# Sparse attention in front of a mixture of experts: mask added by the array, one exponential for all tiles, sums by VectorE, operands built by chunks of features

## The chip, the cores and the metric

One core of one Trainium2 chip. The time is microseconds on the device from the launch to the end of the kernel; the table below has the median of three runs of the kernel before. One execution was profiled: all rows of the trace come from it.

## The reference, cut to what matters

```python
# q, k, v: (4, 8, 576, 64) f32, stride = 32
scores = (1/sqrt(D)) * q @ k^T
mask_local   = (rel >= 0) & (rel < 32)                 # heads 0..3, rel = query position - key position
mask_strided = (rel >= 0) & (kpos % 32 == qpos % 32)   # heads 4..7
scores = where(mask, scores, -1e9); scores -= max(scores); attn = exp(scores)
attn  /= sum(attn) + 1e-9
x = (attn @ v), heads side by side: (2304, 512)
P = exp(x @ w_gate - max); 8 rounds of division by row sums and column sums   # gate, 8 experts
y = sum over experts e of P[:, e] * (relu(x @ w1[e]) @ w2[e])                 # 512 -> 1024 -> 512
out = elu(y @ w_in) @ w_out                                                   # 512 -> 2048 -> 512
```

## The kernel before, in words

**Attention.** The eight heads of a batch are taken in four pairs, two local, two strided, in the order local, strided, local, strided, and each pair is two units: 32 units over the four batches. A unit has 4 to 6 tiles. A local tile has 128 rows (64 queries of two heads) against 96 keys; a strided tile has 108 rows against 54 keys. Only tiles that the mask leaves non-empty are computed; inside a tile the mask is a table of 0 and -1e9 (m_local, m_str). There are 160 tiles in all.

A unit goes through four stages, each a generator: att_s1 (once per pair) turns q and k by TensorE transposes (L425), ScalarE copies q with the scale (L437), VectorE copies k (L443). att_s2 makes the scores of all tiles of a unit in one bank of PSUM (L470: every f32 matmul stands in the trace as two weight loads and two matmuls), VectorE adds the mask on the way to SBUF (L484) and takes the negated maximum (L487). Deferred behind it are exps, one ScalarE exponential per tile with the maximum as bias and the sum accumulated (L491), and norm, two small VectorE operations for the reciprocal (L495, L496) and a GpSimd multiplication of the whole unit (L497). att_s3 transposes the weights in two groups (L511) and copies them out of PSUM (L514 on ScalarE, L516 on VectorE). att_s4 multiplies by v (L529) and VectorE copies the result into x (L549).

The function attention runs a loop over u; in one loop stand att_s2 of unit u-2, a half of att_s1, att_s4 of unit u-5, the other half of att_s1, and the two groups of att_s3 of unit u-4, in this order. After each of these steps the program yields, and a yield counts down the deferred work: exps is written into the program four yields behind its att_s2 (DEF_EXP = 3), norm six (DEF_NORM = 5). Each engine runs its instructions in the order in which they were written; other engines' results are waited for by semaphores. While only attention runs (loops 0 to 20; loops 0 and 1 hold att_s1 alone), nearly every second bank that is opened gets one 512-column matmul on data that nobody reads (warm_up, L341: the first nine banks, then each with n % WARM_MOD < WARM_OF, WARM_MOD = 2).

**Start of the experts.** At u = MOE_FROM = 21 the experts begin, and from there on one step of attention stands in each gap between groups of matmuls. The first layer (gemm1, L923) is a Winograd form of Strassen's product over seven products of quarters. Its operands are made of x's halves: quarters B11 and B21 of the first 512 tokens (build_a), and B22 and the differences T1 to T4 that also need the next 512 tokens (build_b: four VectorE subtractions at L267 for each of two 128-feature chunks, c = 0 and 1). Each operand is split into a high part (ScalarE cast, L277 or L158) and the rest (a subtraction at L168, on VectorE for c = 0 and GpSimd for c = 1 in most of build_b, the other way round in build_a), and a product is three matmuls per chunk. build_a is queued when batch 0's attention is done (batch_done(0), at the end of loop 12); build_b when batch 1's is done, in loop 21, so behind the first step of the experts. A build step is taken at every second yield while attention runs alone, and in each gap later; need(x) in gemm1 writes build steps until operand x is written. The preparation of expert weights (GpSimd sums at L186, casts and subtractions at L158 and L168) begins at yield 66 and takes every second one.

Behind the attention (230 us) the kernel goes on with both layers' matmuls (L923, L1072) to the end; the change touches nothing that is written there but the form of the entries in the set built.

Of the kernel before, what the change touches and what calls it, by code (L numbers as in the profile page):

```python
# [75 lines left out]
def sparse_attention_moe_kernel(ctx: ExitStack, tc: tile.TileContext, a, out):  # L76
# [178 lines left out]
    def build_b(a, b, home=None):  # L255


        hi, lo = xb

        def minus(x, y, i, c):  # L260
            if home:
                out = home(i, c)
            elif i == 4:
                out = y
            else:
                out = hp_.tile([P, HALF], F32, tag="hh" if c else "hl", name="t")
            ve.tensor_tensor(out=out, in0=x, in1=y, op=ALU.subtract)  # L267
            return out

        t1 = [minus(b(c), a(c), 1, c) for c in (0, 1)]  # L270
        yield True
        t2 = [minus(b(c + 2), t1[c], 2, c) for c in (0, 1)]
        yield True

        def both(x, t, engs):
            for c in (0, 1):
                se.copy(hi[:, x, c], t[c])  # L277
            yield True
            for c in (0, 1):
                low(hi[:, x, c], lo[:, x, c], t[c], engs[c])  # L280
            built.add(x)
            yield True

        yield from both(T2, t2, (ve, ve))
        yield from both(T1, t1, (ve, po_))
        t3 = [minus(t2[c], a(c), 3, c) for c in (0, 1)]
        yield from both(T3, t3, (ve, po_))

        t4 = [minus(a(c + 2), t2[c], 4, c) for c in (0, 1)]
        yield from both(T4, t4, (ve, po_))  # L290
        b22 = [b(c + 2) for c in (0, 1)]
        yield from both(B22, b22, (ve, ve))

    def build_plain(src, hi, lo, tmp):
# [158 lines left out]
    def att_s2(u):  # L453
        m, hf = divmod(u, 2)
        local, tiles, nq, nk = geometry(u)
        nt = len(tiles)
        t = pst[m]
        s = ust[u] = {}
        e = s["e"] = at_p.tile([P, 5 * LK], F32, tag="e", name="e_t", bufs=3)[:nq, : nt * nk].rearrange(
            "p (t k) -> p t k", k=nk  # L460
        )
        ng = st_p.tile([P, 6], F32, tag="ng", name="ng")[:nq, :nt]
        sm = st_p.tile([P, 6], F32, tag="sm", name="sm")[:nq, :nt]
        pp = warm_up(abank())
# [12 lines left out]
        s3 = pp[:nq, : nt * nk].rearrange("p (t k) -> p t k", k=nk)  # L477
        if local:
            parts = [(0, 1, m_local[:, 0:1, :])] if hf == 0 else []
            parts.append((len(parts), nt, m_local[:, 1:2, :]))  # L480
        else:
            parts = [(0, nt, m_str[:nq, None, :])]
        for i0, i1, mask in parts:
            ve.tensor_tensor(  # L484
                out=e[:, i0:i1], in0=s3[:, i0:i1], in1=mask.to_broadcast([nq, i1 - i0, nk]), op=ALU.add
            )
        ve.tensor_reduce(out=ng, in_=e, axis=AX.X, op=ALU.max, negate=True)  # L487

        def exps():
            for i in range(nt):  # L490
                se.activation(e[:, i], e[:, i], AF.Exp, bias=ng[:, i : i + 1], accum_out=sm[:, i : i + 1])  # L491

        def norm():
            rc = st_p.tile([P, 6], F32, tag="rc", name="rc")[:nq, :nt]
            ve.tensor_scalar_add(rc, sm, EPS)  # L495
            ve.reciprocal(rc, rc)  # L496
            po_.tensor_tensor(out=e, in0=e, in1=rc[:, :, None].to_broadcast([nq, nt, nk]), op=ALU.mult)  # L497

        defer(DEF_EXP, exps)
        defer(DEF_NORM, norm)  # L500
        yield True

    def att_s3(u):
        local, tiles, nq, nk = geometry(u)
        s = ust[u]
        s["eT"] = at_p.tile([LK, 6 * 2 * SG], F32, tag="eT", name="eT")
        for i0 in (0, 3):
            n = min(3, len(tiles) - i0)
            pt = warm_up(ybank())
            for i in range(n):  # L510
                pe.transpose(pt[:nk, i * nq : (i + 1) * nq], s["e"][:, i0 + i], ident[:nq, :nq])  # L511
            dst = s["eT"][:nk, i0 * nq : (i0 + n) * nq]
            if i0 and not local:
                se.copy(dst, pt[:nk, : n * nq])  # L514
            else:
                ve.tensor_copy(dst, pt[:nk, : n * nq])  # L516
            yield True

    def att_s4(u):
# [57 lines left out]
    def gate_block():  # L577

        for half, parts in enumerate((((B11, 0), (B21, 2)), ((B11, 0), (T1, 0), (B22, 2)))):
            while not all(x in built for x, _ in parts):  # L580
# [53 lines left out]
    def batch_done(b):  # L634

        if b == 0:
            po_.tensor_copy(x1_[:, :, : S - HALF], x0_[:, :, HALF:])
            start_build((0, False, "a"), build_a(lambda c: x0_[:, c, :HALF]))
            gates.append(gate_block())
        elif b == 1:  # L640
            start_build((0, False, "b"), build_b(lambda c: x0_[:, c, :HALF], lambda c: x1_[:, c, :HALF]))
            gates.append(gate_tile(NA // P, x1_[:, :, HALF:]))

    def pair_done(m):

        b, hp = pair_of(m)
        t0 = max(NA, b * S)
        if t0 < (b + 1) * S:
            nc.sync.dma_start(out=x_late[hp][:, t0 - NA : (b + 1) * S - NA], in_=xs[b][hp][:, t0 - b * S :])
        if b > 1:  # L650
            gates.append(gate_pair(b, m % KD, hp))
# [23 lines left out]
        while any(x[0] == key for x in builds):  # L675
            build_step()

    def need(x):
        while x not in built:
            assert builds  # L680
            build_step()

    def attention():
# [1 line left out]
            return stage(u) if 0 <= u < NU else iter(())  # L685

        s1 = iter(())
        for u in range(NU + 5):
# [5 lines left out]
            if u - 5 == 2 * H:  # L694
                batch_done(1)
# [12 lines left out]
            w = u - 5  # L708
# [6 lines left out]
            if w == H - 1:  # L715
                batch_done(0)


    load_qk(0)
# [247 lines left out]
    def gemm1(sg, p, early=False):  # L967
# [356 lines left out]
```

## Time and profile before

| | |
|---|---|
| median of 3 runs | 2082.65 us (2076.6 to 2087.6) |
| the profiled execution's own time | 2084.41 us |
| its span, first to last instruction | 2082.6 us |
| mean granted TensorE clock over the span | 0.986 |
| attention alone | from 9.0 us (first scores) to 95.1 us (first matmul of the experts) |
| attention beside the experts | 95.1 to about 230 us |

Engines: PE = TensorE matmul, PEld = TensorE weight load, DVE = VectorE, ACT = ScalarE, POOL = GpSimd. A PE instruction's end is modelled, so the distance between starts tells more than a duration. The granted clock is 1.00 at the chip's higher TensorE level, 2.4 GHz, and 0.50 at the lower, 1.2 GHz.

### The profile page before, as it was taken

Reading aid. Unit: us, or ns where it says so; the run is one execution under the profiler, and the core shown is the slowest. Engines: PE = TensorE matmul, PEld = TensorE weight load, DVE = VectorE, ACT = ScalarE, POOL = GpSimd, SP = SyncE. Lnnn points to the kernel's source line nnn. Section 1 sums busy time; section 2 is a strip of 40 time slices with the busy share of each in tenths; the row PEclk is TensorE's granted clock in tenths of the full one; section 3 lists DMA queues with packets and bytes.
Section 4 is the critical chain, followed back from the end, with each engine's and each line's share of the span. In section 5 each row is a group of like instructions: output and inputs, shape, how many; then the busy total and the mean of one; then the engine's idle time right before and its main releaser. Section 6 shows DMA issues by size and latency. Waiting matters only on the chain.

```text
span 2082.6 us, 26962 instructions
## 1 busy us (share of the span) xinstructions
PE 2034.9 (98%) x10196; PEld 1687.3 (81%) x10196; DVE 1310.0 (63%) x2165; ACT 743.3 (36%) x1707; POOL 633.7 (30%) x709
## 2 busy tenths in 40 slices
PE   9989999999999999999999999999999989998999
PEld 7767788888888888788888888888888868886887
DVE  5767775645545556666666666666664475557665
ACT  6746333223322323322222222222222354444543
POOL 1422333233333334322222222222222322224231
PEclk8889999999999999999999999999999999999999
DMA  9632121111111213122222222222211101122111
GB/s 179 144 68 74 53 71 51 51 51 55 57 41 51 62 51 111 62 76 85 73 85 73 86 72 86 73 85 73 85 63 44 41 21 41 41 81 91 41 51 51
DMA packets 143378, 143.12 MB, mean 69 GB/s; under 512 B 67328, under 2 KB 106128, under 8 KB 143248
## 3 DMA queue, kind: packets, MB, share of 16 engines
q1 hardware_dynamic: 142288, 141.20, 23.1%
q8 instruction: 80, 1.31, 0.3%
q14 instruction: 50, 0.41, 0.1%
q10 hardware_dynamic: 960, 0.21, 0.1%
HBM read 123.55 MB, written 20.19 MB: 69 GB/s over the span
## 4 chain that ended last, share of the span: by engine, by line
PE 90%; DVE 5%; ACT 4%; issue 1%; POOL 0%; DVEq 0%; ACTq 0%; POOLq 0%
PE ybank L1072 45%; PE bank L923 39%; DVE xl L168 1%; ACT g L946 1%; PE bank L470 1%; ACT g L945 1%; PE ybank L529 1%; PE ybank L511 1%; PE ybank L470 1%; ACT e_t L491 1%; DVE u L982 1%; ACT hh L950 1%; PE bank L425 0%; PE ybank L589 0%; DVE c L982 0%
## 5 line engine op out<-in xcount | busy, mean ns | idle before, releaser
L1072 PE MATMUL ybank<-w2h,hh 128*128 128x512 f32 x1280 | 504.0, 394 | 9.6 <-DVE acc L1089 8.2
L1072 PE MATMUL ybank<-w2h,hl 128*128 128x512 f32 x1280 | 499.2, 390 | 0.0
L1072 PE MATMUL ybank<-w2l,hh 128*128 128x512 f32 x1280 | 499.0, 390 | 0.0
L923 PE MATMUL bank<-xh,w1h 128*128 128x512 f32 x1120 | 443.9, 396 | 10.3 <-DVE u L982 4.8
L923 PE MATMUL bank<-xl,w1h 128*128 128x512 f32 x1120 | 438.1, 391 | 6.1 <-DVE xl L168 6.1
L923 PE MATMUL bank<-xh,w1l 128*128 128x512 f32 x1120 | 436.9, 390 | 0.0
L168 POOL TENSOR_TENSOR w1l<-w1raw,w1h 128x256 fp32r<-128x256 f32 x240 | 207.1, 883 | 449.4 <-ACT w1h L158 449.4
L1103 DVE SCALAR_TENSOR_TENSOR acc<-ybank,prob,acc 128x512 f32<-128x512 f32 x244 | 182.7, 749 | 228.1 <-PE ybank L1072 227.3
L1072 PEld LDWEIGHTS ybank<-w2h,hh 128*128 128x128 f32 x1280 | 240.9, 188 | 61.9 <-DVE acc L1089 11.1
L1072 PEld LDWEIGHTS ybank<-w2h,hl 128*128 128x128 f32 x1280 | 240.9, 188 | 50.4
L1072 PEld LDWEIGHTS ybank<-w2l,hh 128*128 128x128 f32 x1280 | 241.0, 188 | 48.3
L168 POOL TENSOR_TENSOR w2l<-w2raw,w2h 128x512 fp32r<-128x512 f32 x80 | 103.9, 1299 | 567.5 <-ACT w2h L158 552.2
L158 ACT CAST w2h<-w2raw 128x512 fp32r<-128x512 f32 x160 | 97.0, 620 | 470.5 <-issue 406.7
L923 PEld LDWEIGHTS bank<-xh,w1h 128*128 128x128 f32 x1120 | 210.9, 188 | 59.1 <-DVE u L982 6.5
L923 PEld LDWEIGHTS bank<-xl,w1h 128*128 128x128 f32 x1120 | 211.1, 188 | 46.9 <-DVE xl L168 7.8
L923 PEld LDWEIGHTS bank<-xh,w1l 128*128 128x128 f32 x1120 | 210.8, 188 | 44.6
L982 DVE TENSOR_TENSOR u<-bank,a 128x512 f32<-128x512 f32 x160 | 110.6, 691 | 198.6 <-PE bank L923 165.0
L186 POOL TENSOR_TENSOR wsum<-w1raw 128x256 f32<-128x256 f32 x160 | 126.0, 788 | 221.0 <-DMA w1raw<-in_moe_w 156.7
L938 ACT ACTIVATE hh<-bank 128x512 fp32r<-128x512 f32 x192 | 114.0, 594 | 106.2 <-DVE bank L982 103.4
L940 DVE SCALAR_TENSOR_TENSOR hl<-bank,hh 128x512 fp32r<-128x512 f32 x192 | 131.2, 683 | 6.2
L168 DVE TENSOR_TENSOR w1l<-wsum,w1h 128x512 fp32r<-128x512 f32 (+1 forms) x164 | 120.6, 743 | 14.6 <-ACT w1h L158 13.6
L938 ACT ACTIVATE hh<-c 128x512 fp32r<-128x512 f32 x64 | 40.5, 633 | 243.2 <-DVE c L982 243.2
(198 smaller groups left out, 2728.1 us busy)
## 6 DMA issues: line engine op xcount, KB each, us to landing
w1raw<-in_moe_w SPq DMA_DIRECT2D x64, 512.0 KB, 3.5
w2raw<-in_moe_w SPq DMA_DIRECT2D x64, 512.0 KB, 3.5
raw<-in_moe_w_in SPq DMA_DIRECT2D x16, 512.0 KB, 3.9
w_conv<-val SPq DMA_DIRECT2D x32, 256.0 KB, 2.4
raw<-in_moe_w_out SPq DMA_DIRECT2D x16, 512.0 KB, 3.8
w1raw<-w_conv SPq DMA_DIRECT2D x16, 512.0 KB, 4.4
w2raw<-w_conv SPq DMA_DIRECT2D x16, 512.0 KB, 3.7
q_t<-in_q SPq DMA_DIRECT2D x32, 144.0 KB, 3.9
```

Of the source, the lines that this page charges most:

```text
L158: se.copy(hi, src)
L168: eng.tensor_tensor(out=lo, in0=src, in1=hi.bitcast(F32), op=ALU.subtract)
L186: po_.tensor_tensor(out=o, in0=x, in1=y, op=op)
L470: pe.matmul(pp[:nq, i * nk : (i + 1) * nk], q_blk[m % 2][:, qc : qc + nq], t["kT"][:, kc : kc + nk], start=True, stop=True,)
L491: se.activation(e[:, i], e[:, i], AF.Exp, bias=ng[:, i : i + 1], accum_out=sm[:, i : i + 1])
L511: pe.transpose(pt[:nk, i * nq : (i + 1) * nq], s["e"][:, i0 + i], ident[:nq, :nq])
L923: pe.matmul(dst, a_[:, wi, c, :], b_[:, xi, c, :], start=start and i == 0, stop=stop and i == 5, skip_group_check=True,)
L938: se.activation(hh, src, AF.Relu)
L940: ve.scalar_tensor_tensor(out=hl, in0=src, scalar=0.0, in1=hh.bitcast(F32), op0=ALU.max, op1=ALU.subtract)
L982: ve.tensor_tensor(out=out, in0=x, in1=y, op=ALU.add)
L1072: pe.matmul(y, x[:, cs], w[:, f], start=first and f + m == 0, stop=last and f == 1 and m == 2)
L1103: ve.scalar_tensor_tensor(out=at, in0=y, scalar=prob[:, g, e : e + 1], in1=at, op0=ALU.mult, op1=ALU.add)
```

## The change

The mask is added by TensorE: for each tile a matmul of the identity with the mask table opens the accumulation in PSUM, and the score matmul ends it. VectorE takes the maximum from PSUM and subtracts it on the way to SBUF. One ScalarE exponential covers all tiles of a unit and has no accumulator; norm begins with a VectorE sum. All copies behind att_s3 are ScalarE's. exps and norm are deferred by 1 and 3 in place of 3 and 5, att_s3 and att_s4 stand one loop earlier behind att_s2, and the experts begin at u = 20. Every third bank gets the unread matmul. build_a and build_b are queued once per chunk c, as soon as the two head pairs that make up the chunk's features are done: build_a's chunk 0 behind loop 7 and chunk 1 behind loop 11, build_b's chunk 0 behind loop 15 and chunk 1 behind loop 19. A product asks for chunk 0, writes its three matmuls, then asks for chunk 1.

```diff
-    def build_a(src):
+    def build_a(src, cs=(0, 1)):
...
-            yield from splits([(hi[:, x, c], lo[:, x, c], src(c + c0), ve if c else po_) for c in (0, 1)])
-            built.add(x)
+            yield from splits([(hi[:, x, c], lo[:, x, c], src(c + c0), ve if c else po_) for c in cs])
+            built.update((x, c) for c in cs)
...
-        t1 = [minus(b(c), a(c), 1, c) for c in (0, 1)]
+        t1 = {c: minus(b(c), a(c), 1, c) for c in cs}
...
+        masks = [m_local[:, int(x > 0)] if local else m_str[:nq] for x in tiles]
...
-            pe.matmul(
-                pp[:nq, i * nk : (i + 1) * nk],
-                q_blk[m % 2][:, qc : qc + nq],
-                t["kT"][:, kc : kc + nk],
-                start=True,
-                stop=True,
-            )
+            dst = pp[:nq, i * nk : (i + 1) * nk]
+            pe.matmul(dst, ident[:nq, :nq], masks[i], start=True, stop=False)
+            pe.matmul(dst, q_blk[m % 2][:, qc : qc + nq], t["kT"][:, kc : kc + nk], start=False, stop=True)
...
-        for i0, i1, mask in parts:
-            ve.tensor_tensor(
-                out=e[:, i0:i1], in0=s3[:, i0:i1], in1=mask.to_broadcast([nq, i1 - i0, nk]), op=ALU.add
-            )
-        ve.tensor_reduce(out=ng, in_=e, axis=AX.X, op=ALU.max, negate=True)
+        ve.tensor_reduce(out=ng, in_=s3, axis=AX.X, op=ALU.max)
+        ve.tensor_tensor(out=e, in0=s3, in1=ng[:, :, None].to_broadcast([nq, nt, nk]), op=ALU.subtract)
 
         def exps():
-            for i in range(nt):
-                se.activation(e[:, i], e[:, i], AF.Exp, bias=ng[:, i : i + 1], accum_out=sm[:, i : i + 1])
+            se.activation(e, e, AF.Exp)
 
         def norm():
+            ve.tensor_reduce(out=sm, in_=e, axis=AX.X, op=ALU.add)
...
-            if i0 and not local:
-                se.copy(dst, pt[:nk, : n * nq])
-            else:
-                ve.tensor_copy(dst, pt[:nk, : n * nq])
+            se.copy(dst, pt[:nk, : n * nq])
...
+        if b < 2 and m % 2:
+
+            cs = (m % KD // 2,)
+            if b:
+                start_build("b", build_b(lambda c: x0_[:, c, :HALF], lambda c: x1_[:, c, :HALF], cs=cs))
+            else:
+                start_build("a", build_a(lambda c: x0_[:, c, :HALF], cs))
...
-            s2, s3, s4 = of(att_s2, u - 2), of(att_s3, u - 4), of(att_s4, u - 5)
+            s2, s3, s4 = of(att_s2, u - 2), of(att_s3, u - 3), of(att_s4, u - 4)
...
         def prod(dst, wi, xi, start=True):
-            need(xi)
-            for c in products(dst, w, xb, wi, xi, start=start):
+            work = products(dst, w, xb, wi, xi, start=start)
+            for c in (0, 1):
+                need(xi, c)
+                next(work)
...
-WARM0, WARM1, WARM_MOD, WARM_OF, WARM_N = 14, 10, 2, 1, 512
+WARM0, WARM1, WARM_MOD, WARM_OF, WARM_N = 14, 10, 3, 1, 512
-DEF_EXP, DEF_NORM = 3, 5
+DEF_EXP, DEF_NORM = 1, 3
-MOE_FROM, ATT_RATE = 21, 1.1
+MOE_FROM, ATT_RATE = 20, 1.1
```

## Rows read from the trace of the kernel before

**Rows 1.** Section 1 of the page: busy us (share of the span) and instructions per engine

```profile
PE 2034.9 (98%) x10196; PEld 1687.3 (81%) x10196; DVE 1310.0 (63%) x2165; ACT 743.3 (36%) x1707; POOL 633.7 (30%) x709
```

**Rows 2.** Windows: stretch, length, busy PE PEld DVE ACT POOL, clock, DMA, GB/s

```profile
16.00:30.00 14.00, 14.00 (x82) 12.51 (x81) 5.98 (x19) 6.56 (x34) 2.19 (x3) 0.51 0.92 178
...
40.00:55.00 15.00, 14.78 (x178) 12.76 (x177) 11.75 (x32) 12.32 (x53) 3.18 (x4) 1.00 0.96 199
...
66.00:85.00 19.00, 19.00 (x143) 16.49 (x141) 10.98 (x30) 9.63 (x42) 6.74 (x8) 0.55 0.59 123
...
108.00:112.00 4.00, 4.00 (x16) 2.33 (x14) 1.28 (x2) 2.12 (x4) 2.69 (x3) 0.57 0.01 2
...
126.00:140.00 14.00, 13.33 (x70) 8.14 (x69) 5.64 (x15) 5.87 (x18) 1.69 (x3) 0.66 0.37 76
...
230.00:820.00 590.00, 588.90 (x2601) 485.49 (x2600) 340.64 (x554) 182.91 (x367) 201.19 (x239) 1.00 0.18 57
```

**Rows 3.** TensorE's timeline, 40 to 55 us: start, us, instructions, [idle before]

```profile
40.01 1.06 PE L470 MATMUL bank<-kT,q_blk 128*108 128x54 f32 x10
...
54.64 0.48 PE L341 MATMUL bank<-warm 128*128 128x512 f32 x1
...
54.96 1.06 PE L470 MATMUL bank<-kT,q_blk 128*108 128x54 f32 x10
```

**Rows 4.** Chain that ended last, 150 to 182 us: start, us, what, count

```profile
155.17 1.09 PE ybank L470 x10
...
163.49 0.87 PE ybank L470 x8
...
170.94 1.09 PE ybank L470 x12
...
177.78 0.90 PE ybank L470 x10
...
180.41 0.73 PE ybank L529 x20
```

**Rows 5.** TensorE's timeline at the start of attention

```profile
13.04 0.41 PE L425 MATMUL bank<-ident,k_t 96*128 96x96 f32 x3
...
15.70 1.96 PE L470 MATMUL bank<-kT,q_blk 128*108 128x54 f32 x12 [2.25 <-ACT q_blk L437]
```

**Rows 6.** Groups by line, 0 to 230 us: busy us, mean ns, idle before, releasers

```profile
L491 ACT ACTIVATE e_t<-e_t,ng 108x54 f32<-108x54 f32 (+1 forms) x160 | 54.7, 343 | 6.2 <-DVE ng L487 5.6
...
L487 DVE TENSOR_REDUCE ng<-e_t 128x5 f32<-128x480 f32 (+3 forms) x32 | 17.1, 534 | 1.1
...
L516 DVE COPY eT<-ybank 96x384 f32<-96x384 f32 (+3 forms) x48 | 21.3, 459 | 6.1 <-PE ybank L511 5.6
...
L497 POOL TENSOR_TENSOR e_t<-e_t,rc 128x480 f32<-128x480 f32 (+3 forms) x32 | 26.3, 821 | 132.7 <-DVE rc L496 80.8 <-ACT eT L514 8.9 <-ACT w1h L158 8.1
...
L496 DVE RECIPROCAL rc<-rc 128x5 f32<-128x5 f32 (+3 forms) x32 | 6.0, 188 | 1.1
...
L267 DVE TENSOR_TENSOR t<-acc,t 128x512 f32<-128x512 f32 x4 | 2.6, 685 | 0.0
```

**Rows 7.** Timeline of all engines, 60 to 70 us

```profile
61.12 3.38 DVE L168 TENSOR_TENSOR xl<-acc,xh 128x512 fp32r<-128x512 f32 x1
...
63.22 0.73 POOL L186 TENSOR_TENSOR wsum<-w1raw,wsum 128x256 f32<-128x256 f32 x1
...
65.81 0.91 PE L529 MATMUL ybank<-eT,v_t 54*64 54x54 f32 x24 [2.15 <-DVE eT L516]
...
69.29 0.66 DVE L168 TENSOR_TENSOR xl<-acc,xh 128x512 fp32r<-128x512 f32 x1
```

**Rows 8.** Waits, 0 to 230 us: engine, line, waited for: us, times, longest

```profile
PE bank L470 <- ACT e_t L491: 0.9, 1, 0.9
...
PE bank L923 <- DVE xl L168: 6.1, 5, 2.3
...
PE bank L923 <- ACT xh L277: 0.9, 1, 0.9
```

More of the change, by code (lines that the diff above doesn't have):

```diff
@@ L244, in prep_step, with build_b @@
         return False
-    def build_a(src):
+    def build_a(src, cs=(0, 1)):
         hi, lo = xb
         for x, c0 in ((B11, 0), (B21, 2)):
-            yield from splits([(hi[:, x, c], lo[:, x, c], src(c + c0), ve if c else po_) for c in (0, 1)])
-            built.add(x)
+            yield from splits([(hi[:, x, c], lo[:, x, c], src(c + c0), ve if c else po_) for c in cs])
+            built.update((x, c) for c in cs)
             yield True
-    def build_b(a, b, home=None):
+    def build_b(a, b, home=None, cs=(0, 1)):
         hi, lo = xb
@@ L268, in minus @@
             return out
-        t1 = [minus(b(c), a(c), 1, c) for c in (0, 1)]
+        t1 = {c: minus(b(c), a(c), 1, c) for c in cs}
         yield True
-        t2 = [minus(b(c + 2), t1[c], 2, c) for c in (0, 1)]
+        t2 = {c: minus(b(c + 2), t1[c], 2, c) for c in cs}
         yield True
         def both(x, t, engs):
-            for c in (0, 1):
+            for c in cs:
                 se.copy(hi[:, x, c], t[c])
             yield True
-            for c in (0, 1):
+            for c in cs:
                 low(hi[:, x, c], lo[:, x, c], t[c], engs[c])
-            built.add(x)
+                built.add((x, c))
             yield True
@@ L285, in build_b @@
         yield from both(T1, t1, (ve, po_))
-        t3 = [minus(t2[c], a(c), 3, c) for c in (0, 1)]
+        t3 = {c: minus(t2[c], a(c), 3, c) for c in cs}
         yield from both(T3, t3, (ve, po_))
-        t4 = [minus(a(c + 2), t2[c], 4, c) for c in (0, 1)]
+        t4 = {c: minus(a(c + 2), t2[c], 4, c) for c in cs}
         yield from both(T4, t4, (ve, po_))
-        b22 = [b(c + 2) for c in (0, 1)]
+        b22 = {c: b(c + 2) for c in cs}
         yield from both(B22, b22, (ve, ve))
@@ L469, in att_s2 @@
                 qc, kc = x * 2 * NJ, x * NJ
-            pe.matmul(
-                pp[:nq, i * nk : (i + 1) * nk],
-                q_blk[m % 2][:, qc : qc + nq],
-                t["kT"][:, kc : kc + nk],
-                start=True,
-                stop=True,
-            )
-        s3 = pp[:nq, : nt * nk].rearrange("p (t k) -> p t k", k=nk)
-        if local:
-            parts = [(0, 1, m_local[:, 0:1, :])] if hf == 0 else []
-            parts.append((len(parts), nt, m_local[:, 1:2, :]))
-        else:
-            parts = [(0, nt, m_str[:nq, None, :])]
-        for i0, i1, mask in parts:
-            ve.tensor_tensor(
-                out=e[:, i0:i1], in0=s3[:, i0:i1], in1=mask.to_broadcast([nq, i1 - i0, nk]), op=ALU.add
-            )
-        ve.tensor_reduce(out=ng, in_=e, axis=AX.X, op=ALU.max, negate=True)
+            dst = pp[:nq, i * nk : (i + 1) * nk]
+            pe.matmul(dst, ident[:nq, :nq], masks[i], start=True, stop=False)
+            pe.matmul(dst, q_blk[m % 2][:, qc : qc + nq], t["kT"][:, kc : kc + nk], start=False, stop=True)
+        s3 = pp[:nq, : nt * nk].rearrange("p (t k) -> p t k", k=nk)
+        ve.tensor_reduce(out=ng, in_=s3, axis=AX.X, op=ALU.max)
+        ve.tensor_tensor(out=e, in0=s3, in1=ng[:, :, None].to_broadcast([nq, nt, nk]), op=ALU.subtract)
         def exps():
-            for i in range(nt):
-                se.activation(e[:, i], e[:, i], AF.Exp, bias=ng[:, i : i + 1], accum_out=sm[:, i : i + 1])
+            se.activation(e, e, AF.Exp)
         def norm():
+            ve.tensor_reduce(out=sm, in_=e, axis=AX.X, op=ALU.add)
             rc = st_p.tile([P, 6], F32, tag="rc", name="rc")[:nq, :nt]
@@ L579, in gate_block @@
         for half, parts in enumerate((((B11, 0), (B21, 2)), ((B11, 0), (T1, 0), (B22, 2)))):
-            while not all(x in built for x, _ in parts):
+            while not all((x, c) in built for x, _ in parts for c in (0, 1)):
                 yield True
@@ L637, in batch_done @@
             po_.tensor_copy(x1_[:, :, : S - HALF], x0_[:, :, HALF:])
-            start_build((0, False, "a"), build_a(lambda c: x0_[:, c, :HALF]))
             gates.append(gate_block())
         elif b == 1:
-            start_build((0, False, "b"), build_b(lambda c: x0_[:, c, :HALF], lambda c: x1_[:, c, :HALF]))
             gates.append(gate_tile(NA // P, x1_[:, :, HALF:]))
@@ L676, in ready, with need @@
             build_step()
-    def need(x):
-        while x not in built:
+    def need(x, c=0):
+        while (x, c) not in built:
             assert builds
@@ L687, in attention @@
         s1 = iter(())
-        for u in range(NU + 5):
+        for u in range(NU + 4):
             if u % 2 == 0 and u < NU:
@@ L707, in attention @@
                 load_w2(0)
-            w = u - 5
+            w = u - 4
             if w >= 0 and w % 2 == 1:
@@ L714, in attention @@
                 reorder_v(u // 8 + 1, H // 4 + RE_IN.index(u % 8))
-            if w == H - 1:
-                batch_done(0)
+            if w == H - 1 or w == 2 * H - 1:
+                batch_done(w // H)
     load_qk(0)
```

3 lines of the change are left out of this document (removed).

## The prediction

> **What bounds the kernel now.** I read the page's engine section first, then windows, then TensorE's own timeline, the chain and the waits. TensorE is busy for 98% of the span [rows 1], and behind the attention it has no room at all: from 230 to 820 us it is busy for 588.9 of 590 us at full clock [rows 2]. The change reaches only the first 230 us, so its worth there is read from TensorE: work added to it, against waits and slow clock taken away.
>
> While attention runs alone, TensorE is the bound too, at full clock. The scores of two units of the same kind, four loops apart, start at 40.01 and 54.96 us [rows 3]: 3.74 us per loop, with TensorE busy for 14.78 of 15 us, VectorE for 11.75 and ScalarE for 12.32 [rows 2]. A shorter ScalarE or VectorE alone therefore gives nothing in such a loop. What they cost is seen at two places where TensorE stops for over 2 us: from the transposes at 13.04 (done 2.25 us before 15.70) for q_blk, which stood behind the first exponentials on ScalarE [rows 5], and 2.15 us before 65.81 for eT on VectorE [rows 7]. Behind each the granted clock falls to the lower level, 1.2 GHz: 0.51 from 16 to 30 us and 0.55 from 66 to 85 us [rows 2]. That costs 0.49 × 14 = 6.9 us and 0.45 × 19 = 8.6 us. In the experts' first 45 us TensorE waits for the parts of the operands, 6.1 + 0.9 us [rows 8], and the clock gives 0.43 × 4 and 0.34 × 14 = 6.5 us away, from 108 to 112 and from 126 to 140 us [rows 2].
>
> **The change part by part.**
>
> *Masks on TensorE.* The scores of the four kinds of unit take 1.09, 0.87, 1.09 and 0.90 us at full clock [rows 4], 0.99 us in the mean, and a mask matmul has the same shape (stationary 108 or 128 columns, moving 54 or 96, two passes). 32 units × 0.99 = +31.6 us, and TensorE has no idle place that would hide them: 18 units (17.8 us) in the alone stage, 14 (13.8 us) beside the experts. No row shows an identity as f32 weights in an accumulated pair. From below, the narrow v products take 0.73 us for 20 instructions [rows 4], 0.037 each, where the scores take about 0.1: 320 × 0.037 = 11.8 us; from above, I know no reason for more than the scores' price. I take 31.6, the row of the same shape.
>
> *Unread matmuls.* By the program 111 banks are opened in the alone stage, 60 with such a matmul; now 108 and 42. One takes 54.96 − 54.64 = 0.32 us [rows 3]: 18 × 0.32 = −5.8 us. They were work in a bound engine; if their loss opened a slow clock it would cost as below, but the masks put more activity in their place.
>
> *Exponentials, sums, copies.* ScalarE loses 160 activations of 0.34 us [rows 6] and 160 accumulator reads, and gets 32 longer ones and the eT copies. VectorE loses 21.3 us of eT copies and gets 32 sums, priced as the maximum over the same elements, 17.1 us [rows 6]; the subtraction replaces the mask addition, over the same PSUM operand. So VectorE stays at 2.94 − 0.67 + 0.53 = 2.8 us a loop (11.75 / 4 from rows 2, 21.3 / 32 and 17.1 / 32 from rows 6), beside a TensorE loop of now 3.7 + 1.0 − 0.3 = 4.4 us. All of this is hidden: cost 0. What it can free is a wait: 0.9 us for an exponential [rows 8], which I leave out as small.
>
> *Earlier stages.* A unit's chain (maximum 0.53, subtraction about the same, exponential some 0.5, sum 0.53, two small ones of 0.19, GpSimd 0.82: 3.3 us from rows 6) had about two loops before its transposes and now has one, from the scores' end to the end of the next loop, some 6 us. It fits, with 1.5 to 3 us for queueing. In the first loops it does not. There att_s4 is missing, so a loop has too few yields, and norm of unit 0 is written behind unit 1's maximum and subtraction on VectorE. TensorE, which has only two half transposes (0.7 us) to do behind unit 1's scores, waits for 0.53 + 0.53 + 0.53 + 0.38 + 0.82 − 0.7 = 2.1 us and some hand-overs, so 2.1 to 2.6. The old wait of 2.25 us at this place [rows 5] goes (the exponentials no longer hold q_blk), and one of the same length is late in its stead, so I keep the wait and the 6.9 us of slow clock: 0. Bounds: −9 if the clock holds, +2 if the wait is longer.
>
> *The second gap.* eT no longer stands on VectorE behind the 3.38 us subtraction [rows 7], which alone takes 0.66 (the row at 69.29). −2.15 − 8.6 = −10.7 us.
>
> *Operands by chunks.* build_b's chunk 0 moves ahead of the experts, into the last four loops: four subtractions of 0.69 [rows 6] and five of 0.66 [rows 7] = 6.0 us on VectorE, five casts on ScalarE, no DMA. That makes VectorE 2.8 + 1.5 = 4.3 us a loop beside TensorE's 4.4, so it has no slack there. I take 2.5 us of new waits; 0 is the lower bound, and 10.8, four times the blocked subtraction's 3.38 − 0.66 [rows 7], the upper. Beside the experts each build step has half the work, and its last part is asked for one gap later than before, so of the 7.0 us of waits [rows 8] I take 6 back, and of 6.5 us of slow clock 5.5; bounds 0 and 13.5.
>
> The long subtraction ended at 64.5 us, 0.55 behind a GpSimd sum that ran from 63.22 to 63.95 us, about what it takes alone [rows 7]. The Trainium skill's page "SBUF — State Buffer", section "Who interferes with whom", says that a VectorE instruction with two SBUF inputs and a GpSimd instruction that reads SBUF lock each other out for a whole instruction, while one with a single SBUF input does not contend. The trace agrees with the first half (3.38 against 0.66). By it the new subtraction and sums are safe and the nine moved operations are the exposed ones.
>
> *The start at u = 20* moves one unit's scores and half a pair's transposes from the alone stage to the experts': the work is the same.
>
> *Sum:* +31.6 − 5.8 + 0 − 10.7 + 2.5 − 6 − 5.5 = +6.1 us on the profiled execution's 2084.4 (span 2082.6 and 1.8 around it), 2090.5. The median shown is 1.8 us lower than that execution, so on its scale 2088.8; I forecast 2088.
>
> **The rivals.**
>
> *A second slow stretch stays (slower).* In the last four loops the nine subtractions meet GpSimd's weight preparation. VectorE's queue also holds k's copy and the maximum, so one block as at 61.12 us [rows 7] can hold TensorE back. It decides where the block passes the chain's slack and TensorE stops for about 2 us, as at both places before. Price: 2 us and a stretch like 66 to 85, 8.6 us, on top of the sum: 2098. For it: VectorE has no slack there by the sum above. Against: eT has left its queue, and GpSimd's work comes at every second yield only.
>
> *The first slow stretch goes (faster).* If hand-overs are shorter than I think and the first wait stays near 1 us, then 1.2 + 6.9 us less: 2080. For it: the 0.9 us wait [rows 8] left the clock alone. Against: the count above needs 2.1 us without any hand-over.
>
> *Masks nearly free (faster).* If the second matmul of a pair costs half the scores' price, 15.8 us less: 2072. For it: TensorE's narrow v products [rows 4]. Against: those have 64 stationary columns, the identity 108 or 128.
>
> *The stalls do not go.* If the experts' waits and clock remain (other VectorE work is in front of the chunks), the sum is 11.5 higher, 2099; it stands with the first rival.
>
> **How the numbers follow.** Forecast (2088, its own range 2080 to 2095): 0.44. A stretch or the stalls stay (2098): 0.22. First stretch goes (2080): 0.16. Masks cheap (2072): 0.18. About 0.5% (10.4 us) is what a measurement of this kernel can tell from no change, so the borders are 2072.2 and 2093.1. Faster: two thirds of the masks' case and a quarter of the first stretch's, 0.16. Slower: nearly all of the 2098 case, 0.20, and the forecast's upper end, 0.07: 0.27. Within: 0.57. The range 2070 to 2102 leaves out the lower part of the cheap masks and two slow stretches together.
>
> **What would show it.** Scores of a unit with twice the instructions and some 2 us at full clock (half of that more: third rival). A loop of 4.3 to 4.4 us in the middle of the alone stage, against 3.7. One gap of over 2 us near 15 us and about 14 us of clock 0.5 behind it; none near 65 us. The experts' first matmul between 93 and 99 us. Waits of L923 for xl below 1.5 us in all, and a clock of 1.00 from the experts' start to 140 us. Clock below 0.6 anywhere between 40 and 100 us would make the forecast wrong upwards; a clock of 1.00 from the start, or a loop below 4.1 us, downwards.

## The result and the profile after

The change makes the kernel slower: 2098.99 us (median of 5 runs, 2097.82 to 2107.15) against 2079.53 us of the kernel before beside it, ratio 1.0098 [1.008, 1.0116], +19.5 us. The profiled execution took 2102.4 us against 2084.4 before, +18.0; the forecast was +6.1.

Where the time went is seen at four landmarks of the two profiled executions (starts in us):

| | before | after | difference |
|---|---|---|---|
| first matmul of the experts | 95.1 | 101.4 | +6.3 |
| first matmul of the second layer | 154.2 | 160.6 | +6.4 |
| first write of the middle result | 821.9 | 838.1 | +16.2 |
| end of the span | 2082.6 | 2100.6 | +18.0 |

So 6.3 us are lost while attention is alone, none in the experts' first 59 us, and 9.8 us between there and the middle, where nine units' masks stand. A unit's masks cost about 1.04 us by the loops shown below (4.46 - 3.74 + 0.32 for the unread matmul that a loop lost), so nine cost 9.4 us; after also has one unit more than before in that stretch. In the first 59 us five units' masks stand, and shorter waits and less slow clock pay for them. The last 1.8 us lie where the two programs are the same.

Section 1 and the clock line of section 2 of the page of after (busy us, share, instructions; against [rows 1]):

```profile
PE 2058.1 (98%) x10498; PEld 1714.7 (82%) x10498; DVE 1297.3 (62%) x2141; ACT 721.5 (34%) x1467; POOL 629.0 (30%) x709
...
PEclk8999999999999999999999999999999989999999
```

TensorE has 302 matmuls more: 320 for the masks, 18 unread ones fewer. The windows of after (columns as in [rows 2]):

```profile
18.00:38.00 20.00, 19.62 (x122) 17.76 (x123) 5.66 (x17) 4.96 (x12) 2.52 (x4) 0.50 0.54 114
40.00:55.00 15.00, 14.98 (x191) 13.52 (x187) 10.41 (x27) 9.57 (x22) 5.01 (x5) 1.00 0.40 90
66.00:85.00 19.00, 18.97 (x235) 17.02 (x235) 13.75 (x33) 11.39 (x26) 6.63 (x9) 1.00 0.71 148
108.00:112.00 4.00, 3.50 (x34) 2.58 (x31) 2.81 (x7) 2.16 (x5) 0.78 (x1) 1.00 0.83 228
126.00:134.00 8.00, 7.06 (x29) 6.34 (x29) 2.40 (x4) 1.49 (x4) 2.29 (x3) 0.57 0.21 42
```

The slow stretch from 66 to 85 us of [rows 2] is gone, the one beside the experts is shorter (8 us), and the first is longer: 0.50 over 18 to 38 us. TensorE's timeline of after (start, us, what, [idle before]):

```profile
18.38 0.88 PE L500 MATMUL ybank<-ident,e_t 128*96 128x128 f32 x3 [2.61 <-POOL e_t L486]
...
45.80 0.31 PE L472 MATMUL bank<-m_str,ident 108*108 108x54 f32 x2
46.13 0.36 PE L473 MATMUL bank<-kT,q_blk 128*108 128x54 f32 x2
46.33 0.35 PE L472 MATMUL bank<-m_str,ident 108*108 108x54 f32 x2
...
63.63 0.31 PE L472 MATMUL bank<-m_str,ident 108*108 108x54 f32 x2
```

L472 is the mask's matmul, L473 the scores'. A pair of instructions comes every 0.19 us, mask or score (0.22 us for the local tiles). Units start at 45.80 and 63.63 us, four loops apart: 4.46 us a loop, against 3.74 [rows 3]. What TensorE waits for from 97 to 150 us (line, waited for: us, times, longest; against [rows 8]):

```profile
PE bank L912 <- POOL xl L168: 3.0, 2, 2.1
PE ybank L515 <- ACT eT L502: 2.0, 2, 1.3
PE bank L912 <- DVE xl L168: 1.2, 2, 0.7
PE bank L912 <- ACT xh L277: 1.0, 1, 1.0
```

The waits for xl and xh, 7.0 us before [rows 8], are 5.2 us, and most of it is now for GpSimd. The timeline of after around the longest, all engines:

```profile
124.00 0.42 DVE L482 TENSOR_REDUCE sm<-e_t 108x5 f32<-108x270 f32 x1
...
124.67 0.19 DVE L485 RECIPROCAL rc<-rc 108x5 f32<-108x5 f32 x1
...
125.02 0.64 POOL L486 TENSOR_TENSOR e_t<-e_t,rc 108x270 f32<-108x270 f32 x1 [4.47 <-ACT w1h L158]
125.62 1.26 POOL L168 TENSOR_TENSOR xl<-t,xh 128x512 fp32r<-128x512 f32 x1
...
126.94 0.80 PE L912 MATMUL bank<-xl,w1h 128*128 128x512 f32 x1 [2.11 <-POOL xl L168]
```

GpSimd's xl stands behind norm's multiply in its queue, and this starts only when VectorE's sum and reciprocal are done (124.86). The row names ScalarE's w1h, which happened to end at 125.02; but of the 30 multiplies from 28 to 233 us 29 start 0.14 to 0.18 us behind the end of their reciprocal, this one 0.16, so the reciprocal is what it waits for. xl itself takes 1.26 us there, 0.69 on VectorE (the same kind at 95.54 us).

### The profile page after: what moved, and what is told of

Same layout as the page of the kernel before. It is cut to its first block, busy times and chain, and to the rows that moved or that the text cites. A ratio compares the mean times of both kernels' runs of the same rounds, so it can differ in the third digit from the quotient of the medians.

```text
span 2100.6 us, 27287 instructions
## 1 busy us (share of the span) xinstructions
PE 2058.1 (98%) x10498; PEld 1714.7 (82%) x10498; DVE 1297.3 (62%) x2141; ACT 721.5 (34%) x1467; POOL 629.0 (30%) x709
## 4 chain that ended last, share of the span: by engine, by line
PE 91%; DVE 4%; ACT 4%; issue 1%; POOL 0%; DVEq 0%; POOLq 0%; ACTq 0%
PE ybank L1063 44%; PE bank L912 39%; ACT g L935 1%; PE ybank L515 1%; PE bank L473 1%; DVE xl L168 1%; PE bank L472 1%; ACT g L934 1%; PE ybank L473 1%; PE ybank L500 1%; PE ybank L472 1%; DVE u L973 1%; ACT hh L939 1%; PE bank L425 1%; PE ybank L341 0%
## 5 line engine op out<-in xcount | busy, mean ns | idle before, releaser
L1063 PEld LDWEIGHTS ybank<-w2h,hh 128*128 128x128 f32 x1280 | 241.0, 188 | 60.6 <-DVE acc L1080 10.6
L186 POOL TENSOR_TENSOR wsum<-w1raw 128x256 f32<-128x256 f32 x160 | 121.5, 759 | 216.3 <-DMA w1raw<-in_moe_w 141.9
L168 DVE TENSOR_TENSOR w1l<-wsum,w1h 128x512 fp32r<-128x512 f32 (+1 forms) x164 | 121.6, 749 | 14.1 <-ACT w1h L158 13.0
```

What stands on the lines that cost most here:

```text
L168: eng.tensor_tensor(out=lo, in0=src, in1=hi.bitcast(F32), op=ALU.subtract)
L186: po_.tensor_tensor(out=o, in0=x, in1=y, op=op)
L1063: pe.matmul(y, x[:, cs], w[:, f], start=first and f + m == 0, stop=last and f == 1 and m == 2)
```

## The experiments

Each line of a table is one kernel against the kernel before on the same chip. First the change was taken apart into three: M, the masks on TensorE; C, the operands by chunks; R, the rest (subtraction, one exponential, sums on VectorE, copies on ScalarE, stages one unit closer, the constants).

| kernel | parts | us | against before | ratio |
|---|---|---|---|---|
| b_plusmask | M (VectorE's addition kept) | 2091.69 | +12.4 | 1.0058 [1.0046, 1.0071] |
| b_chunk | C | 2072.56 | -6.7 | 0.9969 [0.9957, 0.9981] |
| c_chain | R | 2085.07 | +5.4 | 1.0027 [1.001, 1.0043] |
| c_chunkmask | M, C | 2092.75 | +13.1 | 1.0061 [1.0046, 1.0076] |
| c_nochunk | M, R | 2093.83 | +14.1 | 1.0063 [1.0044, 1.0082] |
| after | M, C, R | 2098.99 | +19.5 | 1.0098 [1.008, 1.0116] |

**b_plusmask.** The mask is added twice here, by both engines.

```diff
+            pe.matmul(dst, ident[:nq, :nq], masks[i], start=True, stop=False)
-            pe.matmul(dst, q_blk ..., t["kT"] ..., start=True, stop=True)
+            pe.matmul(dst, q_blk ..., t["kT"] ..., start=False, stop=True)
```

> The kernel before with the 160 mask matmuls of TensorE added and nothing taken away (VectorE adds the mask once more, which changes no masked weight). If they are plain work on the bound engine, 32 x 1.04 = +33 us: 2114. If half of them fills places where TensorE waits or keeps its clock up, +17: 2098.

+12.4: neither the +33 nor the rival's +17. The experts start at 97.7 us, only 2.6 later than before, with 19 units' masks (19.8 us at 1.04 each) put into the stage in front. Windows of this kernel where [rows 2] has 0.51 and 0.55:

```profile
16.00:30.00 14.00, 13.36 (x129) 12.15 (x129) 6.70 (x23) 8.18 (x37) 3.19 (x4) 0.88 1.05 189
...
66.00:85.00 19.00, 18.65 (x216) 16.68 (x216) 14.96 (x35) 15.14 (x58) 9.31 (x12) 1.00 0.62 127
```

With more work on TensorE the wait for eT at 65 us is covered and the clock stays up there; at the start only some 4 us, from 18 to 22, are partly slow. In this kernel's stage alone the masks are nearly paid for by the slow stretches that went.

**b_chunk.** Only build_a and build_b by chunks, as in the diff of the change.

> The kernel before with only the operands built by chunks. If late operands cost it the 7 us of waits and 6.5 us of slow clock beside the experts, and chunk 1 still waits as in the changed kernel (6.9 us with the slow clock 10.4 in all), 3 to 5 us are gained: 2077 against 2081. If the moved VectorE work makes new waits in the alone stage, where its loop is 3.7 us and VectorE has 2.94 to do before it, 2 us and a slow stretch of 8 are lost: 2090.

-6.7: faster than before and than forecast for it. The gap at 65 us is gone, the experts start at 88.2 us. A part of the rival came as well: a wait of 1.70 us for k at 83 us, with the clock at 0.74 from 80 to 90.

**c_chunkmask, c_nochunk, c_chain.** M and C together; the changed kernel without C; R alone (masks by VectorE everywhere, operands built in one go). The last two keep the products' asking by chunk.

```diff
 # c_nochunk, against after
-        if b < 2 and m % 2: ... start_build(..., cs=cs)
+            start_build("a", build_a(lambda c: x0_[:, c, :HALF]))      # in batch_done(0)
+            start_build("b", build_b(lambda c: x0_..., lambda c: x1_...))   # in batch_done(1)
```

> The kernel before with two parts of the change, the operands by chunks and the 160 mask matmuls (VectorE keeps its own addition, as in the run with the masks alone, so that mask is added twice). Alone they gave -6.7 and +12.4 us. Theory 1, the parts add up and the rest of the change (subtraction, one exponential, sums on VectorE, copies on ScalarE) costs what is missing to +19.5: 2079.5 - 6.7 + 12.4 = 2085. Theory 2, the masks were cheap only because they filled stretches at the lower clock that the chunks take away as well, so that together they cost their full 20 to 25 us: 2092 to 2098, and the rest of the change costs nothing. Over 2090 decides for theory 2.

> The changed kernel with its operands built in one go as before. Theory 1: the chunks are worth what they were worth in the kernel before, 6.7 us, so 2106. Theory 2: with the masks the 65 us gap is covered by them too (it was gone in the run with the masks alone), so the chunks are worth nothing and it stays at 2097 to 2101.

> The kernel before with only the rest of the change: masks added by VectorE, operands built in one go, but subtraction, one exponential, sum by VectorE, copies of e by ScalarE, stages one unit closer. Theory 1: this rest costs some 14 us, 2094. Theory 2: it costs 0 to 4 us, 2079 to 2084; the profile then shows the 65 us gap of before still there and loops of about 3.6 us.

M and C give 13.1, what M gives without C: the chunks' gain is gone once the masks are there, as theory 2 had it. But that theory also said that R costs nothing, and R alone costs 5.4 (theory 1 had 14), while R on top of M and C costs 6.4 (19.5 - 13.1; the intervals of after and c_chunkmask don't meet). On top of M alone it costs 1.7, which the intervals don't separate. And c_nochunk is 5 us faster than after, outside both theories: with M and R the chunks don't gain, they rather cost (the intervals just overlap). C gains where it removes the wait for eT at 65 us and the slow stretch behind it. M removes the same stretch, so their gains are one gain, counted once. c_nochunk's trace has 3.8 us of waits for VectorE's xl, where after has 3.0 for GpSimd's and 1.2 for VectorE's: the chunks moved that wait to another queue instead of ending it.

R alone is not the same R as in after. Since VectorE adds the mask there, the new subtraction reads the scores from SBUF. In c_chain one of them took 3.25 us beside GpSimd's work, and the eT that came behind it stopped TensorE (timeline of all engines, 62 to 71 us):

```profile
65.70 3.25 DVE L489 TENSOR_TENSOR e_t<-e_t,ng 128x480 f32<-128x480 f32 x1
...
69.05 0.60 ACT L492 ACTIVATE e_t<-e_t 128x480 f32<-128x480 f32 x1 [3.16 <-DVE e_t L489]
...
70.44 0.73 PE L528 MATMUL ybank<-eT,v_t 54*64 54x54 f32 x18 [2.44 <-ACT eT L515]
```

In after the subtraction reads PSUM and none takes over 0.66 us. So a part of the 5.4 us belongs to c_chain alone.

**a_nomask.** The changed kernel without the mask matmuls; the scores stay unmasked.

```diff
-            pe.matmul(dst, ident[:nq, :nq], masks[i], start=True, stop=False)
```

> The changed kernel without its 160 mask matmuls: the scores are taken unmasked, all else stays. If TensorE is the bound all through the attention, the masks' 32 units x about 1.04 us (loop of 4.46 us in place of 3.7 + 0.3 less) come back whole, and a little more with the slow stretch at the start: 2099 - 33 = 2066, alone loop 3.5 us. If instead the one-loop chain of VectorE, ScalarE and GpSimd is the bound behind TensorE, the loop stays above 4 us and less than half comes back: about 2085.

2076.68 us, 0.9987 [0.997, 1.0005]: 22 us under after, not 33. TensorE's timeline and a window of it show what the shorter loops (3.5 us) uncover, v's load:

```profile
52.03 1.12 PE L514 MATMUL ybank<-eT,v_t 96*64 96x64 f32 x16 [1.61 <-DMA v_t<-in_v]
```

```profile
50.00:88.00 38.00, 36.30 (x252) 31.79 (x253) 20.14 (x49) 16.32 (x38) 9.61 (x13) 0.51 0.51 114
```

Behind that wait the clock is 0.51 for 38 us.

**a_split and d_beside.** The masks divided: TensorE adds them in the stage alone and VectorE beside the experts (a_split), or the other way round (d_beside).

```diff
+        on_pe = alone_now[0]            # d_beside: not alone_now[0]
+            if on_pe:
+                pe.matmul(dst, ident[:nq, :nq], masks[i], start=True, stop=False)
+        if not on_pe: ... ve.tensor_tensor(out=e[:, i0:i1], in0=s3[:, i0:i1], in1=mask..., op=ALU.add)
```

> The changed kernel with masks by TensorE only while attention runs alone; beside the experts VectorE adds them as before (14 units, 0.5 us each on VectorE, then maximum and subtraction in SBUF). If TensorE is the bound beside the experts, 14 x 1.04 = 14.5 us come back: 2085. If VectorE, which then has 3.3 us a unit there, holds up banks, operands and activations, less than half comes back: 2092 or more.

> The changed kernel with the masks divided the other way round: VectorE adds them in the stage alone (18 units), TensorE beside the experts (14 units). Neither side on TensorE was 2077, only the first side 2085, both 2099. If the two sides add up, this one stands at 2077 + 14 = 2091. If the masks of the stage alone only fill what would be waits or lower clock (as with the masks alone added to the kernel before, +12 of 33), it stands at 2095 to 2099, and the profile shows the lower clock in the loops.

a_split: 2085.35, 1.0025 [1.0006, 1.0044], 13.6 under after, as expected; beside the experts a mask on TensorE is paid in full (14 at 1.04 are 14.6 us). The traces agree: from the experts' first matmul to the first write of the middle result a_split takes 722.8 us (92.45 to 815.21) and after 736.6, 13.9 more. d_beside: 2105.0, 1.0124 [1.0096, 1.0152], over both of its forecasts: instead of 8 us under after it is 6 over (the intervals overlap, so no more than this is shown: TensorE has 18 units' masks less, VectorE has them again, and nothing is gained). TensorE's timeline of d_beside:

```profile
93.25 0.56 PE L528 MATMUL ybank<-eT,v_t 54*64 54x54 f32 x12 [2.07 <-ACT eT L515]
95.08 0.68 PE L528 MATMUL ybank<-eT,v_t 54*64 54x54 f32 x8 [1.27 <-ACT eT L515]
```

and its windows:

```profile
70.00:80.00 10.00, 9.41 (x61) 7.92 (x59) 7.51 (x19) 5.49 (x14) 3.09 (x4) 0.52 0.28 69
80.00:110.00 30.00, 26.46 (x183) 22.16 (x183) 19.46 (x40) 12.84 (x27) 6.95 (x8) 0.61 0.50 115
```

With VectorE's addition back in the unit's chain and less work on TensorE the waits for eT grow (1.22 us at 69 us, 2.07 at 93) and the clock falls to 0.52 and 0.61; after has 1.00 there until 120 us. The experts start 3.9 us earlier than in after (97.6), and the slow clock behind takes that back.

**a_norm2 and a_norm0.** The norm one step earlier, for all units (DEF_NORM = 2) or for the first unit alone.

```diff
-DEF_EXP, DEF_NORM = 1, 3
+DEF_EXP, DEF_NORM = 1, 2                     # a_norm2
-        defer(DEF_NORM, norm)
+        defer(DEF_NORM - (u == 0), norm)     # a_norm0
```

> The changed kernel with the normalization deferred by 2 yields in place of 3, so that in the first loops, which have no v product, it is written ahead of the next unit's maximum. If the 2.61 us wait before 18.38 us is what puts the clock down for 19 us, the wait shrinks to about 1 us, the clock stays at 1.00 there, and 1.6 + 9.6 = 11 us come back: 2088. If the clock falls at the start for another reason, only the 1.6 us: 2097.

> The changed kernel with only unit 0's normalization one yield earlier, so that VectorE has it ahead of unit 1's maximum and, in all later loops, k's copy stays ahead of the sum. In the run with the deferral 2 everywhere the first wait was 1.17 us and the clock stayed at 1.00 there. If that wait alone put the clock down, 1.4 + 9.6 = 11 us come back: 2088. If a slow stretch comes anyway somewhere in the first 60 us, 2097.

In both the first wait is 1.2 us instead of 2.61 and the clock stays at 1.00 behind it, as it would if the wait puts it down; but three other kernels keep the clock up behind the long wait (last section), so that the wait alone is the cause isn't shown. a_norm2 is 2111.54, 1.0149 [1.0131, 1.0167]: norm's sum stands in front of k's copy on VectorE and waits for its exponential in two loops of four, and TensorE stops for k three times, for 1.39 to 1.43 us. TensorE's timeline of a_norm2 and its clock behind:

```profile
37.10 0.36 PE L473 MATMUL bank<-kT,q_blk 128*108 128x54 f32 x2 [1.41 <-DVE kT L443]
```

```profile
10.00:30.00 20.00, 18.84 (x208) 17.27 (x209) 11.43 (x29) 9.52 (x20) 3.19 (x4) 1.00 1.11 201
35.00:45.00 10.00, 8.59 (x65) 7.62 (x64) 4.09 (x12) 3.56 (x10) 1.46 (x2) 0.66 0.36 81
```

a_norm0 is 2094.64, 1.0073 [1.006, 1.0085], 4.4 under after where 11 were expected (the intervals overlap). Its windows:

```profile
10.00:88.00 78.00, 76.08 (x878) 68.91 (x879) 53.51 (x127) 44.73 (x96) 20.58 (x26) 1.00 0.77 157
90.00:100.00 10.00, 9.97 (x50) 8.61 (x48) 5.64 (x13) 4.24 (x9) 2.81 (x3) 0.50 0.74 150
```

The stretch at the start is cured and another follows the waits for eT at 88 to 90 us (0.70 and 1.27 us), which left the clock alone in after.

**a_moe22 and a_warm9.** The experts two loops later (MOE_FROM = 22); no unread matmuls after the start (WARM_OF = 0). In a_moe22 the second expert pair's weights are prepared so early that, as far as the code tells, they replace an operand of the first pair that is still to be used, so part of the first pair's hidden values differ; the amount of work is the same.

> The changed kernel with the experts beginning at u = 22 in place of 20, two loops later: six more build steps of chunk 1 stand ahead of them. If the operands are late because chunk 1 is built only beside the experts, the waits of 101 to 140 us (6.9 us) and the slow clock (3.5 us) go down to a third, for 1.3 us of four more unread matmuls: 2099 - 6 = 2093. If VectorE's and GpSimd's load in that stage is the cause, whatever the order, the waits move and the time stays at 2099.

> The changed kernel with no unread matmul behind the ninth bank: 33 fewer of 0.32 us. If TensorE is the bound in the alone stage and its clock is held by the real work, 10.6 us come back: 2088, a loop of 3.8 us. If they hold the clock, or if VectorE becomes the bound at 2.8 us and more a loop with waits, the clock falls in more places than at the start and the time is the same or longer: 2099 to 2110.

a_moe22: 2096.25, 1.0075 [1.0053, 1.0097]. The waits for xl are gone, but a wait for the gate (1.87 us, ScalarE's lg) and a clock of 0.5 at 95 to 103 and 125 to 132 us stand in their place. a_warm9: 2095.18, 1.007 [1.0043, 1.0097]: the loop falls to between 4.05 and 4.16 us, the time by 4 where 10.6 were expected. The intervals of both overlap that of after, and neither comes near the kernel before.

**d_lowve and d_etve.** The low parts of the chunks on VectorE instead of GpSimd; the copies of eT as before the change.

```diff
-        yield from both(T1, t1, (ve, po_))       # and so for T3, T4
+        yield from both(T1, t1, (ve, ve))        # d_lowve
-            se.copy(dst, pt[:nk, : n * nq])
+            if i0 and not local: se.copy(...)    # d_etve
+            else: ve.tensor_copy(...)
```

> The changed kernel with all low parts of build_b's chunks (six subtractions of 128x512) on VectorE, none on GpSimd. Theory, the masks' stage stalls on GpSimd's queue: there xl stands behind the norm's multiply, which waits for VectorE's new sum; so the waits of 0.84 and 2.11 us and the 3.5 us lost at the lower clock behind the second go: 2099 - 5 = 2093 to 2095. Rival, VectorE becomes late instead: each subtraction is 0.68 us there and the waits for xl come back from VectorE, 2097 to 2101.

> The changed kernel with the transposed e copied as before (VectorE takes the first group and the local tiles, ScalarE the second group). Theory, the copies on ScalarE stand behind casts that wait for VectorE: the waits of 0.69 and 1.27 us for eT at the end of the attention alone go and the time falls by 2 to 4 us, 2095 to 2097. Rival, VectorE is the full engine of that stretch and its copies make kT and the low parts later by as much: 2099 to 2104.

d_lowve (GpSimd has three of the ten low parts of build_b; the six of the expectation is a miscount): 2090.79, 1.0059 [1.0038, 1.0079], 8.2 under after. Its waits from 90 to 150 us, and its window where after has 0.57:

```profile
PE bank L912 <- DVE xl L168: 2.2, 4, 0.9
PE ybank L515 <- ACT eT L502: 1.3, 1, 1.3
PE bank L912 <- ACT xh L277: 1.0, 1, 1.0
```

```profile
126.00:134.00 8.00, 7.39 (x52) 6.41 (x52) 6.02 (x14) 3.59 (x9) 2.41 (x3) 1.00 0.37 104
```

The waits for xl and xh are 3.2 us in place of 5.2, the longest for xl 0.9 us, the clock is 1.00, and the experts' first stage (first matmul to the second layer) takes 54.8 us against after's 59.2: 4.4 us less. The rest of the 8.2 can't be put down to the edit: the profiled execution is the fastest of the eight and has no slow stretch at the start, which the edit does not touch. Their times run from 2086 us at a mean clock of 0.995 to 2098 at 0.988, and at after's clocks of 0.988 and 0.989 they lie 1.5 to 4.4 us under it. d_etve: 2099.83, 1.0097 [1.0074, 1.0121], the rival's case; TensorE then waits 1.46 us for VectorE's eT and 1.05 for ScalarE's, so neither engine's copies are early at the end of the stage alone.

**c_comb and e_repair.** a_norm0 and a_split together, and then d_lowve added.

> The changed kernel with both repairs found so far: the first unit's norm one step earlier (-4.4 alone) and the masks added by VectorE beside the experts (-13.6 alone). If they act at different places they add up: 2099 - 18 = 2081, the same as before. Rival: without masks beside the experts the clock falls at the end of the attention alone as it did in the run with the earlier norm, and that takes back the 4.4 us and more: 2085 or over.

> The changed kernel with all three repairs: first unit's norm a step earlier, masks by VectorE beside the experts, build_b's low parts on VectorE. The first two together were 2079. If the third takes away the waits for GpSimd here too (it gave -8 alone), 2071 to 2074. Rival: beside the experts VectorE now has the masks and the low parts, and the waits for xl come back from it: 2078 to 2082.

2078.95, 0.9993 [0.9979, 1.0007], and 2075.02, 0.9975 [0.9959, 0.999]. The repairs add up (4.4 + 13.6 make 18, and 20 came out), so undoing the change at these two places takes back after's whole loss. The third gave 1.5 more by the differences to before, less than was expected of it, and the intervals don't separate it.

**d_exp0 and e_best.** From b_chunk, the version that gained: the first unit's exponentials and norm two steps later, so that the second pair's q is copied first; then the low parts on VectorE too.

```diff
-        defer(DEF_EXP, exps)
+        defer(DEF_EXP + 2 * (u == 0), exps)      # norm likewise
```

> The kernel before with the operands by chunks (2072.6 us), and the exponentials and the norm of the very first unit two steps later, so that the second pair's q is copied ahead of them. Theory, the first gap (2.27 us for q_blk) starts the slow stretch at 16 us (some 5 us lost): the gap falls to about 1 us, the clock stays at full, 2072.6 - 5 = 2067 to 2069. Rival: the exponentials of two units then stand ahead of the next q copies on ScalarE, the gap comes back at 18 to 22 us, 2071 to 2075.

> The kernel before with the operands by chunks and the first unit's exponentials later (2069.7 us), now also with build_b's low parts on VectorE. Its trace had two waits for GpSimd's xl, 0.84 and 0.99 us, at a clock of 0.93 and 0.90 there. If GpSimd is late there as in the changed kernel: 2066 to 2068. Rival, VectorE, which here adds the masks as well, is as late with them: 2069 to 2072.

d_exp0: 2069.69, 0.9963 [0.9946, 0.998]; e_best: 2065.26, 0.9936 [0.9913, 0.9958], 12 us faster than before and the fastest of all. TensorE's waits in e_best up to 230 us, where [rows 5] has 2.25 for q_blk and [rows 8] 6.1 for xl:

```profile
PE bank L928 <- DVE xl L168: 1.2, 3, 0.8
...
PE bank L470 <- ACT q_blk L437: 1.0, 1, 1.0
```

The clock is 1.00 from the start to 70 us. d_exp0 came out between its two forecasts. Neither d_exp0's step from b_chunk, 2.6 us, nor the last one, 2.7 us by the differences to before, is separated by the intervals.

## Why the prediction was wrong

- **Masks, +31.6: right.** A unit's masks cost about 1.04 us, 33 in all; the 302 instructions agree, and the loop is 4.46 us against 4.3 to 4.4 in the text. Masks nearly free (third rival) is refuted.
- **The first gap: the wait right (2.61 against 2.1 to 2.6), the stretch behind it not a number to carry over.** It took 9.6 us in after's profile where 6.9 were kept: +2.7. In other runs the same wait had other consequences (below).
- **Second gap, -10.7: the number right, the reason not.** There is no wait and no slow clock there. But I credited eT's move to ScalarE. In d_etve VectorE copies eT again, and its window from 66 to 85 us is at 1.00 without a wait; in c_chain ScalarE copies it, and TensorE waits 2.44 us all the same. The blocked subtraction itself is missing in after: no single VectorE instruction between 50 and 88 us takes over 0.76 us, where before one took 3.38. What I did not see is that masks and chunks each earn this gap without the other.
- **New waits in the stage alone, 2.5: about right.** 0.69 + 1.27 = 2.0 us, for eT; 0.67 for k come at 103.20, already beside the experts. In the trace ScalarE's casts of a chunk wait for VectorE's subtraction (3.49 us of idle before the one at 94.88) in front of the copies of eT.
- **The step that failed: beside the experts, "of the 7.0 us of waits I take 6 back, and of 6.5 us of slow clock 5.5".** The waits fell by 1.8, the clock's loss by 3.1 (0.43 x 8 = 3.4 left), so 6.6 us of the saving did not come. I argued that a build step has half the work and looked at VectorE's queue alone. I had worked out that norm gets a VectorE sum but not that GpSimd, which makes three of build_b's ten low parts, has norm's multiply ahead of them. d_lowve takes GpSimd out: the waits fall to 3.2 us and the slow clock there goes. For the waits this shows the cause of the longest one. For the clock it is one trace: c_chunkmask, whose norm needs no VectorE sum, waits 2.4 us for xl and xh, 0.85 at the longest, and ran at 0.57 from 118 to 130 us all the same. So why the clock's share did not come stays open. My rival "the stalls do not go" had the number (2099) partly by luck, since 6.6 of its 11.5 us stayed, and the wrong engine: other VectorE work in front. The 2098 of "a second slow stretch stays" was near by luck too: no such stretch came.
- **"All of this is hidden: cost 0": not shown, and for R as a whole wrong.** R has the unread matmuls too, so by my terms it should have gained; it costs 5.4 us alone and 6.4 on top of M and C. Alone, its trace has a first wait of 3.58 us and the one of 2.44 us at 70 us, with the clock at 0.55 from 70 to 80 (the profiled execution, 2081.2 us, is at the fast end of ten). On top of M and C it puts the first wait of 2.61 us where c_chunkmask has 1.20 at full clock, and raises the waits for xl and xh from 2.4 to 5.2 us. Which of its pieces does how much stays open.

Together: 6.1 + 1.4 (masks) + 2.7 (first stretch) + 6.6 (beside the experts) = 16.8 of the 18.0 us; 1.8 more lie behind 838 us, where nothing differs, so some 0.6 us are the error of this bookkeeping. My signs had it as well: the experts started at 101.4 us and not between 93 and 99, and waited 4.2 us for xl and not below 1.5.

The deeper mistake is that I took the worth of each term from the kernel before with the other terms absent. The masks are 33 us of work and cost 12.4 alone, 22 within the change, 13.6 in the 14 units beside the experts, and, with VectorE's addition in their place, nothing that can be measured in the 18 units alone.

## What to carry to other kernels

Price work that is added to a bound engine by stage: where the stage already loses time to short waits and a lower clock, added work covers them; where every slot is full, it is paid to the last. Two edits that remove the same wait earn it once, so ask of each saving which other part of the change would take it. For a moved operand, look at every engine that makes a part of it, and at what the change puts ahead of it in that engine's queue.

## What the runs showed of the hardware

The slow stretch behind a wait is no fixed price. TensorE's work up to the first gap is the same in after, c_nochunk, a_moe22, a_split, d_lowve and d_etve, and all of them stop there for 2.61 or 2.62 us. Behind it after ran at the lower level from 18.4 to 37.6 us and c_nochunk and a_moe22 from some 20 to 26; the other three kept the higher one up to 38 us. The window of a_split, against after's 0.50:

```profile
18.00:38.00 20.00, 19.92 (x233) 18.13 (x233) 11.60 (x30) 10.63 (x23) 3.54 (x6) 1.00 0.92 169
```

That alone is up to 9.6 us behind the same instructions. The timed executions have no trace, but a mean clock, and within a kernel the time goes with it: a_split's twelve run from 2076.7 us at 0.994 to 2095.6 at 0.983. In which stretch they lost it can't be seen. That the first wait makes this spread isn't shown: d_etve, with it, lies within 3 us, and c_comb, without it, within 9. Nor does a wait's length alone decide: 1.0 to 1.2 us at that place were followed by full clock in a_norm0, c_chunkmask and e_best, but 1.21 us in b_plusmask by 0.72 and 0.50 from 18 to 20 and 20 to 22 us, 1.41 us in a_norm2 by 0.66, and 1.50 us in e_best, at 18 us, by full clock again.
